# First tile's two top levels as one 64x128 matmul for both chunks, with another opening of zeros products

## The chip, the cores and the metric

The kernel runs on one core of one Trainium2 chip. The metric is the time of one execution in microseconds of device time. TensorE multiplies matrices, VectorE (DVE) and ScalarE (ACT) work on elements, GpSimd (POOL) helps with sums and masks, and SyncE (SP) issues most transfers.

## The reference

The inputs r, k, v and w have the shape (4, 8, 768, 48): batch, heads, time, head dimension. A recurrence over time gives y, and its heads side by side are the input of an MLP with an exact GELU.

```python
for t in range(S):
    kt, vt, rt, wt = (k[:, :, t], v[:, :, t], r[:, :, t], w[:, :, t])
    cur = np.einsum('bhd,bhe->bhde', u[None] * kt, vt)
    y[:, :, t] = np.einsum('bhd,bhde->bhe', rt, state + cur)
    state = wt[:, :, :, None] * state + np.einsum('bhd,bhe->bhde', kt, vt)
...
x = attn_out.transpose(0, 2, 1, 3).reshape(B * S, H * D)     # 3072 x 384
h = x @ w_in                                                 # 384 x 2048
g = 0.5 * h * (1.0 + erf(h * inv_sqrt2))
return g @ w_out                                             # 2048 x 384
```

## The kernel before

The work is cut into 8 tiles: four batches by two halves of the time axis, 384 steps each. A tile's attention is worked out in chunks of 64 steps. Inside a chunk, each product r·k with the decay between its two times is built up over levels of h = 1, 2, 4, 8, 16, 32 (`halves`, tiles 1 and 2): at level h the k of the left half of each block of 2h steps meets the r of its right half, then r and k are multiplied by the block's total decays (the updates, L617 and L628, on VectorE), and the block of the product that belongs to this level is copied into `a_sb`. Below h = 16 VectorE copies through a mask (L639); from 16 on ScalarE copies rectangles (L636). The diagonal (with u, prepared by ScalarE at L524) has a product of its own and a masked copy (L588). Updates of a level follow its product, since they overwrite what it reads, and the product of the next level follows the updates.

The first tile is treated alone: its eight heads fall into two units of four (`units[0]`, `units[1]`), each with `np_ = 1` of `NPART = 2` parts, so that unit 0 can start while unit 1's data is on its way. From level 2 on unit 1 goes ahead of unit 0. A level's product is made by `products` (L575): for each of the NI = 6 pairs of chunks, each head half g of the partitions and each chunk p of the pair one matmul of 64x64, whose operands are partitions `half[g]` of k and r and whose result lies in the partitions `half[p]` of a PSUM tile `d`. These are 24 fp32 matmuls. An fp32 matmul stands in the trace as two weight loads and two matmuls, a bf16 one as one of each. Behind the levels come the transposes of k (L798), copied by ScalarE (L800), the products kv (L824), the products of `a_sb` with v (L865), the chain of states on VectorE (L839), the products of r with the states (L894), and the copies into the MLP's input xT (L951, L967 and, over `ysb` with six small transfers, L970 and L886). Then TensorE starts the MLP of the first tile (L1084), interleaved with the second tile's levels.

`keep_warm` (L349) multiplies bf16 zeros into a bank that nobody reads. It opens the kernel with 12 products of 128 columns, followed by two fp32 ones of 512 columns (L353) while the first data is loaded; `products` calls it twice 512 columns behind the diagonals and behind levels 2 and 4 of the first tile, and the stream `warm` six times in the second tile.

The order on each engine is written out by hand: PLAN is a string per tile, whose letters advance streams (generators) of work, "." for unit 0, "s" for unit 1, "f" for the following tile, "l" for loads, "c" and "p" for the weights' conversion. Each engine works in the order in which its instructions were issued, with semaphores between engines; PSUM tiles `d` have three buffers.

Of the kernel before, what the change touches and what calls it, by code (L numbers as in the profile page):

```python
# [10 lines left out]
F32 = mybir.dt.float32  # L11
# [10 lines left out]
C = 64  # L22
# [6 lines left out]
NI = Q * N3  # L29
# [3 lines left out]
BANK = 512  # L33
# [159 lines left out]
def kernel(  # L193
# [9 lines left out]
    nc = tc.nc  # L203
    NX = rkw.shape[0]
    NP = u.shape[1]
    NPART = NP // Q
# [18 lines left out]
    def pair(name):  # L225
        return pools["d"].tile([128, 2, BANK], F32, name=name, tag="d")
# [14 lines left out]
    def bank(name="o_ps", i=None):  # L241
        if i is None:
            i = turns[0]
            turns[0] = 1 - i
        return ps.tile([128, BANK], F32, name=name, tag=f"m{i}")
# [3 lines left out]
    half = [slice(0, 64), slice(64, 128)]  # L249
# [84 lines left out]
    zeros = const.tile([128, BANK], BF16, name="zeros")  # L334
    nc.vector.memset(zeros, 0.0)
    long_zeros = zeros.bitcast(F32).unsqueeze(1).to_broadcast([128, 2, BANK // 2])
    two = const.tile([128, 1], F32, name="two")
# [5 lines left out]
    def keep_warm(n, elsewhere=False, n_cols=BANK):  # L343
        if elsewhere:
            t = pair("warm")[:, 0]
        else:
            t = bank("warm")
        for _ in range(n):
            nc.tensor.matmul(t[:, 0:n_cols], lhsT=zeros[:, 0:128], rhs=zeros[:, 0:n_cols], start=True, stop=True)  # L349

    keep_warm(12, n_cols=BANK // 4)
    for _ in range(2):
        nc.tensor.matmul(bank("warm"), lhsT=zeros[:, 0:2 * 128].bitcast(F32), rhs=long_zeros, start=True, stop=True)  # L353


    masks = {h: const.tile([128, C // 2], U8, name=f"mask{h}") for h in LEVELS if h < 16}
# [37 lines left out]
    for i, h in enumerate(QUARTERS[:1]):  # L394
        for a in range(3):
            w_q = (3 - a) * C // 4
            z = q_ints[1 if a == 0 else 2]
# [81 lines left out]
    def attention(x, unit):  # L479
# [3 lines left out]
        np_ = len(parts)  # L483
# [4 lines left out]
        r, k, w = (bufs[0 if x == 0 or i == 0 and x % 2 == 0 else 1][:, base + i * n_u:base + (i + 1) * n_u]  # L488
                   for i in range(3))
        rc, kc = (z.rearrange("p (b i c t) -> p b i c t", b=np_, c=2, t=C) for z in (r, k))  # L490
# [77 lines left out]
        def products(bs, right, width, warm=True):  # L568
            d = pair("d")
            n = 0  # L570
            for b in bs:
                for i in range(NI):
                    for g in range(2):
                        for p in range(2):
                            nc.tensor.matmul(d[half[p], g, n * width:(n + 1) * width],  # L575
                                             lhsT=kc[half[g], b, i, p], rhs=right(half[g], b, i, p),
                                             start=True, stop=True)
                    n += 1
            if x == 0 and warm:
                keep_warm(2)  # L580
            return d[:, :, 0:n * width]

        def diagonal():
            return [products([b], lambda z, b, i, p: rucs[b][z, i, p], C) for b in range(np_)]

        def copy_diagonal(diag):
            for b in range(np_):
                nc.vector.copy_predicated(out=at[:, :, b * NI:(b + 1) * NI],  # L588
                                          mask=masks[0].unsqueeze(1).unsqueeze(1).to_broadcast([128, 2, NI, C]),
                                          data=diag[b].rearrange("p g (i t) -> p g i t", t=C))  # L590

        def halves():

            for h in LEVELS:
                m = C // 2 // h
                if np_ < NPART:

                    d = products(range(np_), lambda z, b, i, p: rc[z, b, i, p], C, 1 < h < 8)
                    d = d.rearrange("p g (n m two j) -> p g n m two j", two=2, j=h, m=m)[:, :, :, :, 1, :]
                else:  # L600
                    right = rc.rearrange("p b i c (m two j) -> p b i c m two j", two=2, j=h)[:, :, :, :, :, 1, :]
                    d = products(range(np_), lambda z, b, i, p: right[z, b, i, p], C // 2)
                    d = d.rearrange("p g (n m j) -> p g n m j", j=h, m=m)
                if h == 1:
                    yield
                    diag = diagonal()
                yield

                r2 = r.rearrange("p (n two j) -> p n two j", two=2, j=h)[:, :, 1, :]
                t2 = tot[h].rearrange("p (n two) -> p n two", two=2)[:, :, 0:1].to_broadcast(r2.shape)  # L610
                k2 = k.rearrange("p (n two j) -> p n two j", two=2, j=h)[:, :, 0, :]
                tk = tot[h].rearrange("p (n two) -> p n two", two=2)[:, :, 1:2].to_broadcast(k2.shape)
                rk = bass.AP(tensor=r2.tensor, offset=r2.offset, ap=[r2.ap[0], [n_u - h, 2]] + list(r2.ap[1:]))
                tt = bass.AP(tensor=t2.tensor, offset=t2.offset, ap=[t2.ap[0], [1, 2]] + list(t2.ap[1:]))

                def update(z, r2=r2, t2=t2, k2=k2, tk=tk):
                    nc.vector.tensor_mul(*((k2, k2, tk) if z is k else (r2, r2, t2)))  # L617

                if x == 0 and m == 1:

                    update(k)
                    last_r.append(lambda: update(r))
                elif x == 0 and h == 1:
                    update(r)
                    yield
                    update(k)
                else:
                    nc.vector.tensor_mul(rk, rk, tt)  # L628
                yield
                ah = at.rearrange("p g n (m two j) -> p g n m two j", two=2, j=h)[:, :, :, :, 1, :]  # L630
                if h >= 16:

                    for p in range(2):
                        for i in range(m):
                            s = slice(p * 64 + i * 2 * h, p * 64 + i * 2 * h + h)
                            nc.scalar.copy(out=ah[s, :, :, i], in_=d[s, :, :, i])  # L636
                else:
                    mask = masks[h].rearrange("p (m j) -> p m j", j=h).unsqueeze(1).unsqueeze(1)
                    nc.vector.copy_predicated(out=ah, mask=mask.to_broadcast(ah.shape), data=d)  # L639
                if h == 1:  # L640
                    copy_diagonal(diag)
                yield
# [144 lines left out]

        last_r = []
        yield from halves() if x < 2 else quarters()


# [22 lines left out]
        def vs(b, i, g):  # L814
            o = ((parts[b] * NI + i) * 2 + g) * D
            return loaded[x][1][:, o:o + G]

        kvs = []
        for b in range(np_):
            kv_ps = pair("kv_ps")  # L820
            for i in range(NI):
                for p in range(2):
                    for g in range(2):
                        nc.tensor.matmul(kv_ps[half[g], p, i * D:(i + 1) * D], lhsT=k_t(b, i, p, g),  # L824
                                         rhs=vs(b, i, g)[half[p], 0:D], start=True, stop=True)
# [84 lines left out]
        else:  # L910
# [8 lines left out]
            for turn in range(2):  # L919
                for i in range(NI):  # L920
                    for b in range(np_):
                        p = (b + turn) % 2
                        for g in range(2):
                            nc.tensor.matmul(ys[turn][0][b][half[g ^ swap(b)], i * C:(i + 1) * C], lhsT=vs(b, i, g)[half[p]],
                                             rhs=at[half[p], g, b * NI + i, :], start=(i == 0), stop=True, skip_group_check=True)
# [7 lines left out]
            for turn in range(2):  # L933
                ysb = ysb_of() if turn == 0 else ysb
                a = ys[turn][1][:, :, 0:NI * C].rearrange("p b (q i t) -> p b q i t", q=Q, t=C)
                for z in range(2):
                    s = slice(z * G, z * G + D)
# [9 lines left out]
        if split:  # L947
            for c, copy in enumerate((nc.scalar.copy, nc.vector.tensor_copy)):
                for z in range(2):
                    s = slice(z * G, z * G + D)  # L950
                    copy(out=xT[s, 0:Q, :].rearrange("p q (i c t) -> p (q i) c t", c=2, t=C)[:, :, c, :],  # L951
                         in_=ys[0][0][c][s, 0:NI * C].rearrange("p (i t) -> p i t", t=C))
# [3 lines left out]
        for b in reversed(range(np_)):  # L956
            for q in reversed(range(Q)):
# [5 lines left out]
                if which < NJ:  # L963
                    for z in range(2):
                        s = slice(z * G, z * G + D)
# [291 lines left out]

    def warm():
        for _ in range(2):
            keep_warm(3, True)  # L1260
            yield

    def masks_and_sums():
# [6 lines left out]
    for x in range(NX):  # L1270
        following = attention(x + 1, 0) if x + 1 < NX else iter(())
        if x == 0:
            streams = {
                ".": units[0], "s": units[1], "f": following, "c": pieces_of_w, "w": next_v(), "x": warm(),
                "p": prepare_apart(),
                "l": chain(weight_in(0, True), islice(second, 5), weight_in(1, True), second, weight_in(2, True)),
            }
        else:
            streams = {
                **(mlp(x - 1) if x > 1 else {".": first_mlp()}),  # L1280
                "s": slots, "f": following,
                "l": load(x + 1, nc.sync),
                "x": sums_of_x(x),
                "w": masks_and_sums() if x == 1 else chain(h_sums([1]), o_sums(EARLY, len(FORMS_O))) if x == 2 else iter(()),
                "y": o_sums(0, EARLY) if x == 1 else iter(()),
                "c": pieces_of_w if x == 1 else iter(()),
            }
        for c in PLAN[x]:
            next(streams[c], None)
        for c in ".slxwp" if x == 0 else ".slxwcy" if x == 1 else ".vgeoslxw":  # L1290
            while next(streams[c], streams) is not streams:
                pass
        slots = following
        if x == 1:
            fewer_pairs()
# [63 lines left out]
```

## Time and profile before

| what | value |
|---|---|
| three timed runs | 575.67, 576.38, 577.77 us; median 576.38 |
| the profiled execution | 577.52 us, span 575.7 us, granted clock 1.00 |
| TensorE matmuls | busy 551.3 us (96%), 7412 instructions |
| TensorE weight loads | busy 491.1 us (85%), 7420 instructions |
| VectorE | busy 489.2 us (85%) |
| ScalarE | busy 334.1 us (58%) |
| first product of the MLP (L1084) | starts at 42.58 us |
| opening, L349 and L353 | 1.19 to 6.17 us |

Times in the trace count from the start of the span. A matmul's record includes a fixed time to drain, so that records of a dense row overlap; how often they start is their pace. PE is TensorE's matmul row, PEld its row of weight loads.

### The profile page before, as it was taken

The page shows a single profiled execution, that of the slowest core. Times are in us where ns is not written, and L with a number is a line of the kernel's source. Part 1 is how long each engine was busy: PE and PEld are TensorE (multiplying, and loading weights), DVE is VectorE, ACT ScalarE, POOL GpSimd, SP SyncE. Part 2 cuts the span into 40 slices and gives each one's busy share as a digit, 9 for nine tenths or more (in the row PEclk, how much of TensorE's full clock was granted, in tenths as well). Part 3 has the DMA queues.
Part 4 walks back from the last instruction along what each step waited for, and adds up shares of the span by engine and source line. Part 5 has one row for each costly group of instructions (what it writes and reads, how often), then busy time and mean ns, then how long its engine had stood idle before and what let it go on. Part 6 is the DMA issues. An engine that isn't in the chain of part 4 may idle for free. (4 is left out here: it accounts for less than half of the span.)

```text
span 575.7 us, 17712 instructions
## 1 busy us (share of the span) xinstructions
PE 551.3 (96%) x7412; PEld 491.1 (85%) x7420; DVE 489.2 (85%) x977; ACT 334.1 (58%) x768; POOL 106.1 (18%) x105
## 2 busy tenths in 40 slices
PE   7689999999998999999999999999999999999997
PEld 4576665689998989999898998989898988999997
DVE  7889879999989989798989979799888989755464
ACT  2468995347753677347763477527772478535820
POOL 5100000016200460006400252005500072000000
PEclk9999999999999999999999999999999999999999
DMA  8559742239342782558623593337915384200001
GB/s 303 178 159 370 239 142 87 81 86 154 47 82 64 175 106 36 139 156 131 81 46 114 135 165 44 60 91 159 131 30 135 84 105 62 43 25 30 0 1 41
DMA packets 71646, 62.15 MB, mean 108 GB/s; under 512 B 32912, under 2 KB 56720, under 8 KB 71568
## 3 DMA queue, kind: packets, MB, share of 16 engines
q1 hardware_dynamic: 50112, 45.62, 26.4%
q0 software_dynamic: 21216, 15.34, 20.3%
q8 instruction: 58, 0.95, 0.7%
q14 instruction: 20, 0.16, 0.1%
q10 hardware_dynamic: 240, 0.08, 0.1%
HBM read 36.24 MB, written 4.72 MB: 71 GB/s over the span
## 5 line engine op out<-in xcount | busy, mean ns | idle before, releaser
L1148 POOL DMA_DIRECT2D g<-o_sb x78 | 94.9, 1490 | 370.7 <-ACT g L1117 347.2
L1197 DVE TENSOR_TENSOR g<-g 128x512 f32<-128x512 f32 x112 | 75.1, 688 | 24.3 <-PE o_ps L1073 21.3
L1117 ACT COPY o_sb<-u_ps 128x384 f32<-128x384 f32 (+1 forms) x56 | 25.8, 461 | 67.6 <-PE u_ps L1073 66.2
L1073 PE MATMUL h_ps<-forms_x,w_in_sb 128*128 128x192 f32 x280 | 57.7, 332 | 0.0
L1073 PE MATMUL o_ps<-w_out_sb,g 128*128 128x192 f32 x280 | 50.5, 327 | 0.5 <-DVE g L1197 0.5
L1117 ACT COPY g<-h_ps 128x384 f32<-128x384 f32 x84 | 40.4, 482 | 16.3 <-PE h_ps L1073 14.4
L1073 PEld LDWEIGHTS h_ps<-forms_x,w_in_sb 128*128 128x128 f32 x280 | 46.6, 190 | 2.7 <-ACT g L1117 2.2
L1073 PEld LDWEIGHTS o_ps<-w_out_sb,g 128*128 128x128 f32 x280 | 46.0, 190 | 1.2 <-DVE g L1197 0.8
L1166 ACT ACTIVATE g<-g 128x384 f32<-128x384 f32 x98 | 46.2, 519 | 0.3
L1073 PE MATMUL o_ps<-t,g 128*128 128x192 f32 x224 | 41.4, 328 | 0.1
L726 ACT COPY a_sb<-d 32x320 f32<-32x320 f32 (+5 forms) x108 | 39.3, 364 | 3.6 <-DVE a_sb L784 1.7
L1073 PEld LDWEIGHTS o_ps<-t,g 128*128 128x128 f32 x224 | 36.8, 190 | 0.7 <-PE u_ps L1073 0.3
L1073 PE MATMUL h_ps<-forms_x,s 128*128 128x192 f32 x168 | 35.5, 334 | 0.0
L1073 PE MATMUL h_ps<-xT,w_in_sb 128*128 128x192 f32 x168 | 35.0, 331 | 0.1
L710 PE MATMUL d<-kx,rkw 64*64 64x96 f32 x1152 | 32.0, 248 | 3.0 <-ACT a_sb L726 1.9
L710 PEld LDWEIGHTS d<-kx,rkw 64*64 64x64 f32 x1152 | 25.6, 133 | 9.6 <-issue 4.3
L1084 PE MATMUL h_ps<-xT,w_in_sb 128*128 128x384 f32 x96 | 33.0, 494 | 0.2
L1073 PE MATMUL u_ps<-xT,w_in_sb 128*128 128x192 f32 x168 | 32.5, 328 | 0.1
L1073 PE MATMUL u_ps<-w_out_sb,g 128*128 128x192 f32 x168 | 30.9, 332 | 1.4 <-ACT o_sb L1115 0.8
L1092 PE MATMUL o_ps<-w_out_sb,g 128*128 128x384 f32 x96 | 31.7, 489 | 0.0
L575 PEld LDWEIGHTS d<-rkw 64*64 64x64 f32 x1152 | 19.1, 134 | 14.2 <-issue 8.5
L739 DVE COPY_PREDICATED a_sb<-quarter,d 128x480 f32<-128x480 uint8 (+5 forms) x54 | 23.2, 440 | 8.7 <-PE d L710 7.4
(178 smaller groups left out, 1206.2 us busy)
## 6 DMA issues: line engine op xcount, KB each, us to landing
g<-o_sb POOLq DMA_DIRECT2D x78, 192.0 KB, 4.2
rkw<-in_rkw_dram SPq DMA_DIRECT2D x54, 256.0 KB, 3.7
raw<-in_w_out_dram SPq DMA_DIRECT2D x8, 768.0 KB, 5.4
v_in<-in_v_dram SPq DMA_DIRECT2D x8, 584.0 KB, 4.6
out_dram<-o_sb SPq DMA_DIRECT2D x24, 192.0 KB, 2.1
raw<-in_w_in_dram SPq DMA_DIRECT2D x5, 768.0 KB, 9.2
rkw<-kx SPq DMA_DIRECT2D x72, 48.0 KB, 2.1
rkw<-in_rkw_dram SPq DMA_DIRECT2D x6, 384.0 KB, 6.8
```

The lines of the kernel that those rows point to most:

```text
L575: nc.tensor.matmul(d[half[p], g, n * width:(n + 1) * width], lhsT=kc[half[g], b, i, p], rhs=right(half[g], b, i, p), start=True, stop=True)
L710: nc.tensor.matmul(d[half[p], g, i * 3 * C // 2:(i + 1) * 3 * C // 2], lhsT=kc[half[g], n // NI, n % NI, p], rhs=rx[half[g], 2 * n + p], s ...
L726: nc.scalar.copy(out=at[z, g, first:behind, (a + 1) * h:], in_=d[z, :, :, to] if g == slice(None) else d[z, :, to])
L739: nc.vector.copy_predicated(out=an[:, :, :, :, (a + 1) * h:], mask=mask.to_broadcast(data.shape), data=data)
L1073: nc.tensor.matmul(o, lhsT=lhsT, rhs=rhs, start=start, stop=True, skip_group_check=True)
L1084: nc.tensor.matmul(h_ps, lhsT=w_in_sb[:, f // FI, j, f % FI * 128:(f % FI + 1) * 128], rhs=xT[:, j, :], start=(j == 0), stop=(j == NJ - 1))
L1092: nc.tensor.matmul(o, lhsT=gs[f // FG][:, f % FG, i * 128:(i + 1) * 128], rhs=w_out_sb[:, f, :], start=(f == 0), stop=(f == NF - 1))
L1117: nc.scalar.copy(out=o, in_=z)
L1148: nc.gpsimd.dma_start(out=o, in_=saved[q, t], accum_op=ALU.add)
L1166: nc.scalar.activation(out=o, in_=z, func=AF.Gelu, scale=MINUS.get(h, 1.0))
L1197: nc.vector.tensor_add(o, o, g_block(what[3:5]))
```

## The change

It has three parts.

The opening: instead of 12 bf16 products of 128 columns and two fp32 products of 512 columns, one fp32 product of 512 columns and then 59 fp32 products of 64x64 zeros, which go round the four quarters of the array in the order of the real products.

The two top levels of the first tile: for h = 16 and 32, `products_of_both` makes one matmul for both chunks of a pair. Its stationary operand is the k of both chunks (128 columns), its moving operand the right halves of r of both (64 columns). A unit's level takes 12 matmuls of 64x128 instead of 24 of 64x64. Half of each result belongs to k of one chunk and r of the other, and is not read; ScalarE's copies pick the matching chunk `p`.

The warming: `products` warms only behind the diagonals, no more behind levels 2 and 4, and the second tile's six warming products have 64 columns instead of 512.

```diff
-    keep_warm(12, n_cols=BANK // 4)
-    for _ in range(2):
-        nc.tensor.matmul(bank("warm"), lhsT=zeros[:, 0:2 * 128].bitcast(F32), rhs=long_zeros, start=True, stop=True)
+    nc.tensor.matmul(bank("warm"), lhsT=zeros[:, 0:2 * 128].bitcast(F32), rhs=long_zeros, start=True, stop=True)
+    small = zeros.bitcast(F32)
+    t = [bank("warm") for _ in range(2)]
+    for i in range(59):
+        g, p = half[i // 2 % 2], half[i % 2]
+        nc.tensor.matmul(t[i // 2 % 2][p, 0:64], lhsT=small[g, 0:64], rhs=small[g, 64:128], start=True, stop=True)
...
+        def products_of_both(h):
+            d = pair("d")
+            for i in range(NI):
+                for g in range(2):
+                    right = r[half[g], i * 2 * C:(i + 1) * 2 * C].rearrange("p (m two j) -> p m two j", two=2, j=h)[:, :, 1, :]
+                    nc.tensor.matmul(d[:, g, i * C:(i + 1) * C], lhsT=k[half[g], i * 2 * C:(i + 1) * 2 * C], rhs=right,
+                                     start=True, stop=True)
+            return d[:, :, 0:NI * C].rearrange("p g (n c m j) -> p g n c m j", c=2, j=h, m=C // 2 // h)
...
-                if np_ < NPART:
-
-                    d = products(range(np_), lambda z, b, i, p: rc[z, b, i, p], C, 1 < h < 8)
+                both = np_ < NPART and h >= 16
+                if both:
+                    d = products_of_both(h)
+                elif np_ < NPART:
+
+                    d = products(range(np_), lambda z, b, i, p: rc[z, b, i, p], C, False)
...
-                            nc.scalar.copy(out=ah[s, :, :, i], in_=d[s, :, :, i])
+                            nc.scalar.copy(out=ah[s, :, :, i], in_=d[s, :, :, p, i] if both else d[s, :, :, i])
...
-            keep_warm(3, True)
+            keep_warm(3, True, 64)
```

## The prediction

> **What bounds the kernel now.** I read the page first. TensorE is busy 96% of the span, and the table of stretches shows where the rest is:
>
> ```profile
> 42.60:110.00 67.40, 67.22 (x945) 42.94 (x942) 61.35 (x98) 53.87 (x80) 0.00 (x0) 1.00 0.53 184
> ```
>
> The first number after the stretch is its length, the next TensorE's busy time: from 42.6 us on TensorE has no holes to speak of, so the end of the kernel moves by as much as the first product of the MLP (L1084, at 42.58) moves. All that is changed runs before it. There TensorE has holes, and the timeline calls the larger ones "issue", a wait for nothing that the profile shows:
>
> ```profile
> 13.19 0.80 PE L575 MATMUL d<-rkw 64*64 64x64 f32 x38 [0.24 <-issue]
> ...
> 18.12 0.45 PE L575 MATMUL d<-rkw 64*64 64x64 f32 x11 [1.46 <-issue]
> ...
> 22.68 1.39 PE L575 MATMUL d<-rkw 64*64 64x64 f32 x80 [0.61 <-issue]
> ...
> 33.98 0.86 PE L865 MATMUL y_ps<-a_sb,v_in 64*64 64x64 f32 x44 [1.39 <-issue]
> ...
> 37.71 1.59 PE L575 MATMUL d<-rkw 64*64 64x32 f32 x94 [0.57 <-issue]
> ```
>
> Two lines of the page explain them:
>
> ```profile
> PE 551.3 (96%) x7412; PEld 491.1 (85%) x7420; DVE 489.2 (85%) x977; ACT 334.1 (58%) x768; POOL 106.1 (18%) x105
> ...
> q8 instruction: 58, 0.95, 0.7%
> ```
>
> A queue named "instruction" moves 58 packets, 0.95 MB, so 16 KB each; 7412 matmuls and 7420 weight loads over 58 packets are 256 instructions a packet. The stretches between the ends of those holes hold just that many (x after PE and PEld; an instruction across a border counts twice):
>
> ```profile
> 13.19:18.12 4.93, 3.18 (x125) 2.35 (x128) 4.75 (x9) 2.94 (x3) 3.67 (x7) 1.00 0.83 258
> 18.12:22.68 4.56, 3.40 (x125) 2.48 (x127) 3.69 (x9) 0.00 (x0) 0.00 (x0) 1.00 0.71 234
> 22.68:26.41 3.73, 2.32 (x129) 2.17 (x128) 3.58 (x7) 2.15 (x7) 0.00 (x0) 1.00 0.26 72
> 26.41:30.25 3.84, 3.49 (x126) 3.13 (x126) 2.77 (x7) 2.48 (x7) 0.00 (x0) 1.00 0.72 217
> ```
>
> So TensorE's program arrives in blocks of 256, one in use and one ahead: the trace starts a packet 1.1 to 1.4 us after a hole ends (2.1 to 2.4 while the DMA share is over 0.7), it takes 0.9 to 1.4 us, and the next block runs 1.2 to 1.5 us later. One block thus takes 3.7 us in quiet, 4.6 to 5.2 under load, while TensorE could run 256 such instructions in 1.9 us (48 matmuls and 48 loads in 0.93 less a drain of 0.22). Blocks begin at instruction 187 (run at 8.04) and then every 256, released at 13.19, 18.12, 22.68, 26.41, 30.25, 33.98, 37.71, 41.30. Beside this, VectorE is nearly full from 8 to 18 us. Past 36 us the path goes over ScalarE:
>
> ```profile
> 36.10 0.48 ACT L970 COPY ysb<-y_ps 128x384 f32<-128x384 f32 x1 [1.79 <-PE y_ps L894]
> 36.61 2.20 ACTq L886 DMA_DIRECT2D xT<-ysb  x3
> 38.90 0.96 ACT L951 COPY xT<-y_ps 48x384 f32<-48x384 f32 x2 [2.32 <-DVE xT L951]
> 39.87 2.14 ACT L524 ACTIVATE kx<-rkw,u_sb 128x384 f32<-128x384 f32 x4
> ```
>
> It waits for unit 1's states (L894), and these stand behind unit 0's y product, which the hole before 33.98 holds up.
>
> **The change in instructions.** An fp32 matmul is two loads and two matmuls, a bf16 one a load and a matmul. The opening grows from 12x2 + 2x4 = 32 to 4 + 59x4 = 240: plus 208. Four pairs of warming matmuls go (16), and four products (levels 16 and 32, two units) shrink from 24x4 to 12x4 (192): minus 208. From the transposes (L798) on, every block therefore begins where it did; before that, all of them fall earlier in the work:
>
> - 443: was 16 instructions into level 2's first product, now 5 into unit 1's level 1.
> - 699: was in level 4's first product, now 65 of 96 into level 2's first.
> - 955: was in level 8's second, now 33 into level 4's second.
> - 1211: was at level 32's first, now at level 16's first.
>
> **Opening.** TensorE starts at 1.19. The one long product takes two of the four records that now fill 2.44 to 6.17, 1.9 us. A small product's record takes 14.6 ns at the pace of L575; before 6.5 us the trace runs at half pace (128-column bf16 every 107 ns, 512-column ones later every 216), so 29 ns, 118 records in 3.4 us: done at 6.5, before the data (6.93). Cost 0, or 0.3 if each takes a tenth longer.
>
> **Blocks.** Instruction 187 is now the 46th small product, at 5.8 instead of 8.04. Before, 5.15 us lay between it and block 443, so 10.9; the fetch looks some 64 instructions ahead (in unbroken runs a packet starts 0.6 us after its border, not 1.1), worth 0.4 us more among slow products: 10.6. Unit 1's level 1 loses 1.1 us (its data allows 9.51). VectorE feels it at the k update (L617), which follows the diagonal product: 12.3 for 11.60, plus 0.7. Level 2's first product starts at 13.2, stops at instruction 699 until 10.6 + 4.93 = 15.5 and ends at 16.0; its update (L628) starts at 16.05 for 14.34, plus 1.7. Then VectorE works its queue off without the 0.15 and 0.46 us waits of before: level 4's first update at 19.55 for 18.66, plus 0.9. Block 955 comes at 15.5 + 4.56 = 20.1, level 4's second update at 20.85 for 20.03, plus 0.8; level 8's second 24.1 for 23.43; level 16's second 26.3 for 25.65, plus 0.65. Block 1211 (20.1 + 3.73 = 23.85) stops nobody, so level 32's first product, held until 26.41 before, starts at 26.45 behind its update and is done at the same 27.35. What was lost early is paid back here: at 28 us the shift is 0, within 0.1.
>
> The gain comes behind it. Block 1467 is there at 27.6 instead of 30.25. The fetch passes that border at about 29.0, while the kv products (L824) still wait for ScalarE, so block 1723 comes at 29.0 + 3.7 = 32.7 for 33.98. Unit 0's y product ends at 33.5, unit 1's states take 1.17 + 0.22: L970 at 35.0 for 36.10, minus 1.1. If L951 really waits for VectorE's L951 (38.89), which follows unit 0's states and the chain that ends at 35.43, only 0.8 of it comes through. I take **minus 0.9**.
>
> **Width.** No row has 64x128 fp32. Two such products fit beside each other where four 64x64 did, so 24 records of 58.3/2 ns are the same 0.70 us. That is one bound; 54.4 ns each (half the 108.7 between the 128-column transposes of L798), 1.31 us, is the other, and it would delay levels 16 and 32, in series on each unit, by 0.6 each, 1.05 where VectorE does not cover it. Below 0.70 the 58.3 ns excludes. I take 0.70, the nearest row in partitions and moving columns. The Trainium skill ("TensorE: Matmul & The Clock Gate", LDWEIGHTS) says that a load's time goes by its columns, P/1.2 ns; by it the loads would set 1.28 us and the sum become about plus 0.1. The rows of 64 and 128 columns (133 and 190 ns) go that way but not in proportion.
>
> **Rest at nothing.** The four removed warming pairs (about 0.5 us each) lay beside waits for blocks or VectorE: 0 to minus 0.1. Tile 2's six narrower ones stand ahead of diagonal products that wait for L524 until 42.02: 0. ScalarE's copies (L636) keep shape and number.
>
> **Sum.** The profiled execution took 577.52 (span 575.7 and 1.8 around it): minus 0.9 is 576.6. It lay 1.1 above the median of 576.38, which becomes **575.5**. A measurement can tell about 0.5%, 2.9 us, from no change.
>
> **Rivals.**
> - *128-column loads set the pace*: plus 1.05 on the sum, 576.5. For it the 190 ns row; against it that loads overlap matmuls all over the trace. 0.17.
> - *The first block comes later still*: the DMA engines are full from 2.7 to 15 us, and the first packet of before was the slowest. Half a us more, and a fetch that does not run ahead of waiting instructions (no gain at 33.98): 576.9. 0.15.
> - *It doesn't do what I say*: the holes are no fetches, so moving instructions moves none; only the warming is saved, 576.3. The Trainium skill ("Runtime: NRT & Kernel Launch", Instruction fetch mechanics) supports that: the next 16 KB page is fetched during the current one and crossing a border is "mostly hidden". The counts of 256 above speak against hidden. 0.08.
> - *More gain*: the first packet starts after 1.2 us as in quiet. Block 443 then stops nobody and the later ones come 1.2 us earlier: 574.2 or, with VectorE's waits gone too, 573.0. 0.16.
> - *Slower: TensorE falls back to half pace.* Between 13.7 and 20.1 us it now has holes of 1.9 and 2 us and no warming between. All through before, the granted clock stays 1.00 over holes of up to 1.5 us. It decides if some 3 us hold too little work: then about 5 us of products on the path between 20 and 37 us double, 575.5 + 5 = 580.5. The Trainium skill (same clock page, Part 1) closes the gate after one idle window of about 3.4 us; no run here has shown that, and no hole reaches it. 0.08.
>
> **Numbers.** The forecast has 0.36. The range of 573.2 to 577.9 holds it and all rivals but the last and the far end of more gain, with the spread of the runs (575.67 to 577.77) around the ends. Faster by over 0.5% (below 573.5) is half of "more gain", 0.08; slower (above 579.3) is half pace and a little for an unseen cost, 0.09; within, 0.83.
>
> **What would show it.** Right: holes that end near 10.6, 15.5 and 20.1, none before level 32, the y hole ending near 32.7, L970 at 35.0, L1084 at about 41.7. Wrong: holes still at 13.2 and 18.1 (no fetches), L636's products over 1 us (loads), L575 records 29 ns apart after 15 us (clock), or L1084 at 42.6 or later.

## The result, and the profile after

The change made the kernel slower: 581.52 us median of 9 runs (579.46 to 583.32) for 576.38 (575.39 to 578.82, 9 runs), a ratio of 1.0081 with a 95% interval of 1.0059 to 1.0104. The forecast was 575.5 with a range of 573.2 to 577.9. The profiled execution took 583.02 us (span 581.2); its mean granted clock (the share of TensorE's full speed that it was given) was 0.994, and 0.992 over the nine runs, where before's profile had 1.000. A border, below, is the place between two blocks of 256 instructions.

TensorE's timeline of the changed kernel, at the places that answer to the holes shown before (start, length, work; in brackets the idle time ahead of it and what ended that; L578, L880 and L1099 are L575, L865 and L1084 of before, L591 is the new product):

```profile
11.44 0.86 PE L578 MATMUL d<-rkw 64*64 64x64 f32 x43 [1.75 <-issue]
...
18.04 3.38 PE L578 MATMUL d<-rkw 64*64 64x64 f32 x110 [3.54 <-issue]
...
26.33 5.60 PE L591 MATMUL d<-rkw 64*128 64x64 f32 x96 [0.31 <-DVE rkw L643]
...
37.22 0.86 PE L880 MATMUL y_ps<-a_sb,v_in 64*64 64x64 f32 x44 [0.91 <-issue]
...
45.09 2.15 PE L578 MATMUL d<-kx,rkw 64*64 64x64 f32 x69 [0.47 <-issue]
47.16 3.21 PE L1099 MATMUL h_ps<-xT,w_in_sb 128*128 128x384 f32 x7
```

The second hole starts 34 matmul records into unit 1's level 2, where the prediction put instruction 699, but it ends at 18.04 and not at 15.5. Level 2's first update on VectorE follows it at 18.87. First the changed kernel, then before:

```profile
18.87 0.96 DVE L643 TENSOR_TENSOR rkw<-rkw,tot_sb 128x768 f32<-128x768 f32 x1 [3.22 <-PE d L578]
```

```profile
14.34 0.97 DVE L628 TENSOR_TENSOR rkw<-rkw,tot_sb 128x768 f32<-128x768 f32 x1
```

Of this delay of 4.5 us only a part is won back. The transposes of k start 3.7 us late (31.86 for 28.16), and ScalarE's rows stand 3.2 us behind those of before:

```profile
39.34 0.48 ACT L985 COPY ysb<-y_ps 128x384 f32<-128x384 f32 x1 [1.30 <-PE y_ps L909]
...
43.12 2.13 ACT L527 ACTIVATE kx<-rkw,u_sb 128x384 f32<-128x384 f32 x4
```

Between that row and the MLP's first product another 1.3 us is lost: 47.16 for 42.58 is 4.6. The stretches by the clock's own edges show what else happened (length, TensorE's busy time, ..., the clock last but two):

```profile
14.45:17.86 3.41, 0.05 (x1) 0.00 (x0) 1.17 (x3) 2.63 (x3) 1.48 (x4) 1.00 0.65 196
17.86:21.27 3.41, 3.23 (x110) 3.16 (x110) 2.16 (x5) 0.00 (x0) 0.00 (x0) 0.50 0.18 36
41.76:45.17 3.41, 1.99 (x92) 1.63 (x88) 3.21 (x8) 3.00 (x6) 0.00 (x0) 1.00 0.56 156
45.17:48.58 3.41, 3.41 (x71) 2.71 (x71) 2.78 (x6) 2.98 (x4) 0.00 (x0) 0.50 0.98 305
```

The clock was halved twice, each time for 3.41 us: behind the hole (0.05 of 3.41 us busy), and again behind a stretch that was busy for 1.99 of 3.41 us, in which TensorE waited for L527 and for a block. The second time takes the diagonal products and the first of the MLP (45.17 to 48.58). Behind the MLP's start TensorE is as full as before, and the rest of the loss there is small: the distance to before is 4.75 us when the MLP's second product starts (L1107, 90.51 for 85.76) and 5.5 at the end, after one stop at 407 us (1.14 us, a wait for ScalarE) that before's profile does not have.

### The profile page after: what moved, and what is told of

It reads as the page before. It is cut to its first block, busy times and chain, and to the rows that moved or that the text cites. A ratio compares the mean times of both kernels' runs of the same rounds, so it can differ in the third digit from the quotient of the medians.

```text
span 581.2 us, 17720 instructions
## 1 busy us (share of the span) xinstructions
PE 555.3 (96%) x7420; PEld 497.2 (86%) x7420; DVE 488.6 (84%) x977; ACT 333.2 (57%) x768; POOL 105.2 (18%) x105
## 4 chain that ended last, share of the span: by engine, by line
PE 68%; DVE 11%; issue 8%; ACT 7%; DMA 3%; SPq 1%; POOL 1%; ACTq 0%; DVEq 0%; POOLq 0%
PE u_ps L1088 18%; PE o_ps L1088 16%; PE h_ps L1088 11%; PE h_ps L1099 6%; PE o_ps L1107 5%; PE d L578 3%; ACT a_sb L741 3%; PE d L725 2%; DMA rkw<-in_rkw_dram 2%; DVE a_sb L754 2%; PE kv_ps L839 2%; PE y_ps L909 1%; PE y_ps L939 1%; DMA g<-o_sb 1%; DVE a_sb L799 1%
## 5 line engine op out<-in xcount | busy, mean ns | idle before, releaser
L1132 ACT COPY g<-h_ps 128x384 f32<-128x384 f32 x84 | 40.2, 480 | 16.5 <-PE h_ps L1088 14.5
L1099 PE MATMUL h_ps<-xT,w_in_sb 128*128 128x384 f32 x96 | 33.4, 500 | 0.0
L1107 PE MATMUL o_ps<-w_out_sb,g 128*128 128x384 f32 x96 | 31.7, 489 | 0.0
L1088 PEld LDWEIGHTS h_ps<-forms_x,s 128*128 128x128 f32 x168 | 27.7, 190 | 3.8 <-ACT u_ps L1132 3.8
```

The lines of the kernel that those rows point to most:

```text
L1088: nc.tensor.matmul(o, lhsT=lhsT, rhs=rhs, start=start, stop=True, skip_group_check=True)
L1099: nc.tensor.matmul(h_ps, lhsT=w_in_sb[:, f // FI, j, f % FI * 128:(f % FI + 1) * 128], rhs=xT[:, j, :], start=(j == 0), stop=(j == NJ - 1))
L1107: nc.tensor.matmul(o, lhsT=gs[f // FG][:, f % FG, i * 128:(i + 1) * 128], rhs=w_out_sb[:, f, :], start=(f == 0), stop=(f == NF - 1))
L1132: nc.scalar.copy(out=o, in_=z)
```

## The experiments

Fourteen kernels, each beside runs of the kernel before on the same chip (576.6 to 577.7 us median there). Clock is the mean granted clock over the runs; one stretch of 3.41 us at half pace lowers it by 0.0029. The kernel before did not always keep its clock either: of its 94 runs beside these kernels 31 had 0.997 or less, and the mean by chip was 0.998 to 1.000. The last columns come from each kernel's one profile: level 2's first update, and the MLP's first product.

| kernel | us (runs) | ratio, 95% interval | clock | level 2 update | MLP start |
|---|---|---|---|---|---|
| before (its profile) | 577.52 (1) | | 1.000 | 14.34 | 42.58 |
| the change | 581.52 (9) | 1.0081 (1.0059 to 1.0104) | 0.992 | 18.87 | 47.16 |
| opening only | 582.81 (7) | 1.0088 (1.0055 to 1.0122) | 0.993 | 17.89 | 47.89 |
| 64x128 products only | 580.56 (12) | 1.0055 (1.0028 to 1.0081) | 0.998 | 14.23 | 42.87 |
| less warming only | 576.72 (12) | 0.9970 (0.9947 to 0.9994) | 0.996 | 14.76 | 44.53 |
| change, old opening | 580.53 (11) | 1.0053 (1.0019 to 1.0086) | 0.993 | 14.41 | 41.58 |
| fp32 opening of 32 instructions | 578.29 (10) | 1.0003 (0.9979 to 1.0027) | 0.998 | 14.26 | 44.05 |
| change, fewer zeros | 588.17 (1) | | 0.988 | 16.13 | 47.89 |
| change, loads held | 586.99 (1) | | 0.985 | 15.72 | 49.64 |
| opening, four loads later | 581.38 (10) | 1.0075 (1.0048 to 1.0101) | 0.994 | 15.61 | 45.98 |
| change, old opening, borders restored | 589.73 (1) | | 0.983 | 14.09 | 49.46 |
| short opening, less warming | 579.37 (1) | | 0.997 | 13.95 | 42.51 |
| narrow later warming only | 578.73 (12) | 1.0019 (0.9993 to 1.0045) | 0.997 | 14.21 | 42.15 |
| no warming at levels 2 and 4 only | 577.31 (12) | 0.9984 (0.9954 to 1.0014) | 0.995 | 14.11 | 41.13 |
| change, filled hole | 583.75 (6) | 1.0103 (1.0077 to 1.0128) | 0.997 | 17.52 | 44.89 |
| opening, filled hole | 583.10 (12) | 1.0084 (1.0056 to 1.0113) | 0.997 | 17.78 | 48.31 |

**Which part costs the time.** The first four take the change apart.

Opening only:

```diff
+    nc.tensor.matmul(bank("warm"), ..., rhs=long_zeros, ...)
+    for i in range(59): ...                       # small zeros products, as in the change
     # warming and 64x64 products as before
```

> The kernel before with the new opening alone (59 small zeros products, all warming kept, 64x64 products at every level). Theory A (the opening adds 208 instructions, so every border between instruction blocks of 256 comes earlier in the work, while the fetches cannot come earlier because the first loads hold the DMA engines until about 15.6 us): TensorE stands from about 14.3 to 18 us as after the whole change, level 2's first update comes at 18.5 to 19 us instead of 14.3, the granted clock halves for 3.4 us behind the hole, the first MLP product starts at 45.5 to 47 us instead of 42.6, and the time is 579 to 581 us. Rival R1 (the clock and the wait come from the warming taken out): no half pace, 576 to 577 us. Rival R2 (the 64x128 products cost it): 576 to 577 us.

Measured 1.0088, all of the loss and a little above Theory A's numbers (582.81 us, MLP start 47.89). The hole and the clock are much like those of the whole change, although all warming is kept:

```profile
13.55 0.79 PE L578 MATMUL d<-rkw 64*64 64x64 f32 x34
17.07 0.70 PE L578 MATMUL d<-rkw 64*64 64x64 f32 x14 [2.73 <-issue]
```

```profile
13.33:16.75 3.42, 0.90 (x35) 0.65 (x34) 2.12 (x5) 2.40 (x3) 2.81 (x8) 1.00 0.73 236
16.75:20.16 3.41, 2.73 (x63) 2.02 (x65) 0.97 (x2) 0.42 (x1) 0.00 (x0) 0.50 0.35 96
```

Warming could not help: its instructions stand behind the same border.

64x128 products only:

```diff
-                if np_ < NPART:
+                both = np_ < NPART and h >= 16
+                if both:
+                    d = products_of_both(h)
+                elif np_ < NPART:
```

> The kernel before with one 64x128 product for both chunks at levels 16 and 32, opening and warming as before. Theory A: the borders up to level 16 stay where they were, nothing before level 16 moves; each of the four products takes 1.26 us instead of 0.70, of which between 0 and 2.2 us in all reach the MLP's start; 192 instructions fewer move the later borders; no half pace; 576 to 578.5 us. Rival R2: the products are the loss, 579 to 582 us. Rival R1: 576.4 us.

The time is what R2 expected (580.56), above Theory A's range. But in the profile the products themselves are little of the loss: level 2 is where it was and the MLP starts 0.3 us late. The profiled run (579.54 us) ends 2.0 us behind before's, so most of that lies behind the MLP's start (below).

Less warming only:

```diff
-                    d = products(..., C, 1 < h < 8)
+                    d = products(..., C, False)
-            keep_warm(3, True)
+            keep_warm(3, True, 64)
```

> The kernel before without the warming behind levels 2 and 4 and with 64 columns in the second tile's six warming products. Theory A: holes end at 13.2 and 18.1 us as before and stay below 3.4 us, so the clock does not fall at 18 us; around 41 to 45 us TensorE may fall to half pace once for 3.4 us, worth up to 1.7 us; 576 to 578 us. Rival R1 (the missing warming behind levels 2 and 4 lets the clock fall at 18 us): half pace between 18 and 22 us, 578 to 581 us.

It is the only kernel here whose interval lies below 1, by 1.7 us at the middle and next to nothing at the end. The clock did halve once in its profile, at 13.63 us; Theory A had it fall, if at all, at 41 to 45 us. The MLP starts 1.95 us late in this profile, and 1.4 us of that is gone by the end: what is lost ahead of the MLP does not pass on whole in every kernel.

The change with the old opening:

```diff
-    nc.tensor.matmul(bank("warm"), ..., rhs=long_zeros, ...)
-    for i in range(59): ...
+    keep_warm(12, n_cols=BANK // 4)
+    for _ in range(2): nc.tensor.matmul(bank("warm"), ..., rhs=long_zeros, ...)
```

> The changed kernel with the old opening (12 bf16 products and two long fp32 ones): 64x128 products and less warming stay. Theory A: the first borders are back where they were, the hole ends at 18.1 us after less than 2 us, no half pace there; level 2's first update at 14.3 to 14.5 us; what stays is the 64x128 products' 0.56 us each and at most one half-paced stretch at 42 to 46 us: 576 to 579 us. Rivals R1 and R2 (warming, width): the loss stays, 580 to 582 us.

The front is as Theory A has it (update at 14.41, MLP 1.0 us earlier than before), the time is that of the rivals. Its runs spread with the clock: 577.58 and 578.50 us at 0.997 and 1.000, 585.19 and 586.02 at 0.985 and 0.984. So the parts other than the opening have costs of their own; they come out under "The loss behind the front".

**Number or kind.** An opening of fp32 zeros only, as long as the new one, with 32 instructions:

```diff
-    keep_warm(12, n_cols=BANK // 4)
     for _ in range(2): nc.tensor.matmul(bank("warm"), ..., rhs=long_zeros, ...)
+    for i in range(6):
+        nc.tensor.matmul(t[i // 2 % 2][p, 0:256], lhsT=small[g, 0:64], rhs=small[g, 0:256], ...)
```

> The kernel before with an opening of fp32 zeros products only, as long as the new one but of 32 instructions as the old one: two of 512 columns and six 64x64 quarters of 256 columns. Theory A (it is the 208 instructions): all borders stay, holes end at 13.2 and 18.1 us as before, first MLP product at 42 to 43.5 us, granted clock 0.997 or more; ratio 0.998 to 1.003. Rival R3 (the kind of product, fp32 zeros in place of bf16, leaves TensorE slower or the clock lower): first MLP product at 46 to 48 us, ratio 1.006 to 1.011.

The hole is shorter than before's, and the ratio is 1.0003: fp32 zeros do no harm, 208 more instructions do.

```profile
17.63 0.45 PE L579 MATMUL d<-rkw 64*64 64x64 f32 x11 [0.92 <-issue]
```

(The MLP's start, 44.05, lies outside what was expected; one half-paced stretch behind the y hole, at 36.05 us, is in this profile.)

The change with 124 instructions fewer:

```diff
+    nc.tensor.matmul(bank("warm"), ..., rhs=long_zeros, ...)      # a second long one
-    for i in range(59):
+    for i in range(27):
```

> The changed kernel with 27 small zeros products instead of 59 and a second long one in their place: about the same TensorE time in the opening, 124 instructions fewer. Theory A (number of instructions and the loads): border 699 lies 124 instructions later in the work, the second packet still starts at 14.5 to 15.7 us and its block runs at 17 to 18.2 us, so that the hole ends where it ended but begins about 2 us later (about 16 us), is shorter than 2.5 us, and the clock does not halve behind it; level 2's first update at 14 to 15 us, first MLP product at 42 to 44 us; 576 to 580 us. Rival R3 (the kind of product in the opening, not their number, is what counts): hole from 14.3 to 18 us, half pace, first MLP product at 46 to 48 us, 580 to 583 us.

The time, 588.17 us, fits neither theory, and the MLP's start, 47.89, is where Rival R3 had it. Block 699 stopped TensorE for only 0.15 us, and the update came at 16.13 instead of 18.87. But the clock halved earlier (at 12.13, in the first hole, which ends at 12.46), the borders behind the levels now fell into the products y and with the states (holes up to 34.41 and 37.86 us), and half pace followed from 42.85 to 53.09 us. It is a single run, which ends 10.7 us behind before's profile: moving borders moves the holes, and fewer instructions alone are not a remedy.

**What holds the packet.** The trace's instruction queue gives when a packet starts, the timeline when its block runs:

| kernel | first packet, block runs | second packet, block runs |
|---|---|---|
| before | 10.88, 13.19 | 15.62, 18.12 |
| the change | 9.00, 11.44 | 15.56, 18.04 |
| opening only | 8.88, 11.28 | 14.55, 17.07 |
| change, loads held | 8.89, 11.05 | 12.21, no stop |
| opening, four loads later | 9.13, 11.44 | 12.60, 15.02 |
| opening, filled hole | 8.75, 11.20 | 13.41, no stop |

```diff
-    0: "l.s....llsl.lssslslss.lc.l.slslls...
+    0: ".s....s.ssssss.llllllllc.l.slslls...       # the change, loads held
+    0: "l.s....lls.ssssss.lllllc.l.slslls...       # opening only, four loads later
```

> The changed kernel with the first eight loads of weights and of the second tile moved behind the levels in the first tile's order; nothing else moves. Theory A (the loads hold the second packet back): the second packet starts 1.1 to 1.5 us after the first hole's end (12.3 to 13.3 us) instead of 4.1 us, its block runs by 15.0 to 16.0 us, level 2's first update comes at 15.5 to 16.5 us, and no window of 3.4 us is empty, so no half pace at 18 us. The time itself may well be worse, since the weights come later. Rival R4 (the packets are late for a reason of their own, such as a fixed time after the border): second packet at 15.5 us and hole to 18 us as after the change.

> The kernel before with the new opening (240 instructions), and the second tile's first four loads issued a few steps later in the first tile's order. Theory A (new opening moves the borders up, the loads hold the packet): the second packet starts at 12.3 to 13.5 us instead of 14.6, its block runs by 16 us instead of 17.1 us, level 2's first update at 15 to 16.5 us; the window in which the clock was lost is used more, so the half pace at 16.7 us goes in most runs; first MLP product 1.5 to 4 us earlier than with the opening alone (47.9 us), ratio 1.000 to 1.006. Rival R4 (late for a reason of its own): as the opening alone, ratio 1.007 to 1.011, first MLP product at 47 to 48 us.

With the loads out of the way the second packet starts 1.2 us after the end of the first hole, as in quiet stretches, and with the loads held level 2 runs through:

```profile
14.00 2.29 PE L578 MATMUL d<-rkw 64*64 64x64 f32 x96
```

With the loads in place, over all kernels, it starts 1.6 to 4.1 us after the hole. So Theory A's packet is shown, against R4. But the time did not come back in either: 1.0075 is R4's range (its MLP start, 45.98, is Theory A's), and the first, a single run, though the clock no longer fell at 18 us, lost it at 12.03 and at 25.68. In the second kernel the loads that were moved met the next packet but one:

```profile
15.02 0.45 PE L578 MATMUL d<-rkw 64*64 64x64 f32 x14 [0.53 <-issue]
...
25.00 1.24 PE L578 MATMUL d<-rkw 64*64 64x64 f32 x37 [2.22 <-issue]
```

```profile
21.04:24.45 3.41, 1.25 (x72) 1.01 (x62) 2.58 (x5) 0.00 (x0) 0.00 (x0) 1.00 0.94 285
24.45:27.86 3.41, 2.86 (x104) 2.86 (x103) 2.30 (x4) 0.95 (x4) 0.00 (x0) 0.50 0.66 220
```

The packet started late (22.78 us, DMA share 0.94), the hole moved from level 2 to a later level, and with it the half pace.

**Late block or half pace.** Four long zeros products ahead of unit 1's level 2 give TensorE something to do in the hole:

```diff
+                if x == 0 and h == 2 and unit == 1:
+                    for _ in range(4):
+                        nc.tensor.matmul(bank("warm"), ..., rhs=long_zeros, ...)
```

The first has it on the change, the second on the opening alone, in place of the warming at levels 2 and 4, so that no later border moves.

> The changed kernel with four fp32 zeros products of 512 columns (16 instructions, about 3.5 us of TensorE) ahead of unit 1's level 2, so that the hole in front of the late block is filled with work that nobody needs. The block comes no earlier. Theory A1 (the late block itself is most of the loss, the half pace behind it a small part): TensorE still stops short of 18 us, level 2's first update at 18.2 to 18.9 us, no half pace there; first MLP product at 46 to 47.2 us for 47.16; ratio 1.005 to 1.009. Theory A2 (the half pace behind the hole is most of it): first MLP product at 42.5 to 45 us, ratio 0.999 to 1.004.

> The kernel before with the new opening, and with the four warming pairs behind levels 2 and 4 replaced by four fp32 zeros products of 512 columns ahead of unit 1's level 2: as many instructions as with the opening alone, but TensorE has work in the hole. Theory A1 (the late block itself is the loss): half pace at 16.7 us gone, granted clock 0.997 or more in most runs, and still ratio 1.005 to 1.009, first MLP product at 45 to 47.5 us. Theory A2 (the half pace behind the hole is the loss): ratio 0.999 to 1.004, first MLP product at 42.5 to 45 us.

The second kernel's timeline and stretch:

```profile
13.18 3.60 PE L600 MATMUL warm<-zeros 128*128 128x512 f32 x8
16.71 1.63 PE L578 MATMUL d<-rkw 64*64 64x64 f32 x96
```

```profile
13.77:17.18 3.41, 3.41 (x38) 1.46 (x40) 1.59 (x3) 2.86 (x3) 2.38 (x7) 1.00 0.66 172
```

The half pace at 17 us is gone in both, and the loss stays (1.0103 and 1.0084). On the change, three runs at a clock of 0.999 to 1.000 still took 581.67, 583.50 and 583.68 us. (In the first two, some 1 us more than in the others lies outside the span, which is 579.0 and 580.5 us.) The twelve runs of the second have a mean clock of 0.997, hardly below the 0.998 of before's runs beside them. So a level 2 that starts at 16.5 or later costs time with the clock kept. It is not shown that the late block alone would: the packet came earlier in these two (13.39 and 13.41), and the filling itself stood in the way until 16.45 and 16.71. Both MLP starts, 44.89 and 48.31, lie outside the numbers of Theory A1 (46 to 47.2, 45 to 47.5), and the first, inside A2's, was not followed by A2's time.

**The loss behind the front.** The 64x128 products alone leave out 192 instructions (with the old opening and less warming, 208), and every later border falls elsewhere. First the 64x128 kernel, then before, at the first tile-2 products of r with the states:

```profile
102.24 1.57 PE L906 MATMUL y_ps<-rkw,st 64*64 64x64 f32 x95
105.03 0.21 PE L906 MATMUL y_ps<-rkw,st 64*64 64x64 f32 x1 [1.21 <-issue]
```

```profile
101.59 1.58 PE L894 MATMUL y_ps<-rkw,st 64*64 64x64 f32 x96
103.10 4.14 PE L1092 MATMUL o_ps<-w_out_sb,g 128*128 128x384 f32 x12
```

A border now falls on the last product of a row of small ones, and TensorE stands for a block. It does so again at 245, 378 and 510 us; before has its own such stops, at other places (178 and 445 us). On TensorE, this profile is 0.6 us behind before at 88 us, 2.1 behind after the first of these stops, and 2.0 behind at the end. To test it, 208 instructions of zeros went into the first MLP of the change with the old opening:

```diff
         for f in range(NF):                      # first MLP, 13 of its 16 block rows
+            for p in 2 * half if f < 13 else ():
+                nc.tensor.matmul(t[p, T:T + 64], lhsT=small[half[0], 0:64], rhs=small[half[0], 64:128], ...)
             for j in range(NJ):
```

> The changed kernel with the old opening, and 52 zeros products of 64x64 (208 instructions) spread over the first 13 block rows of the first MLP: every border from 80 us on lies where it lay before. Theory A (the loss of the two runs with the old opening and 64x128 products comes from borders that fell into later rows of small products): from 100 us to the end this kernel keeps its distance to the kernel before within 0.7 us, without the steps of 0.5 to 1.5 us at 102, 242 to 246, 375 and 505 us; first MLP product at 41.5 us, the added products take 1 to 3 us; 576 to 578.5 us. Rival R5 (those steps are accidents of a run): steps of such size stay, at other places, 577.5 to 581 us.

From 123 us to the end its distance to before goes from 12.0 to 12.2 us. The border stops at 102, 245, 378 and 510 us are gone; the row that stopped at 105.03 now runs through:

```profile
113.55 1.58 PE L908 MATMUL y_ps<-rkw,st 64*64 64x64 f32 x96
```

One step of 1.4 us remains near 236 us, a wait for VectorE, which others give back. It is one profile. What was not foreseen is the front, and with it the time (589.73): MLP start at 49.46. Here the clock halved at 19.44 and stayed so for 17.07 us, through all four 64x128 products (line, engine, tile: shortest, median and longest record in ns):

```profile
L590 PEld LDWEIGHTS d<-rkw x96: 283/331/331, 22.9 to 32.9; 64*128 64x128 f32 x96
```

```profile
22.86:33.10 10.24, 10.24 (x99) 10.23 (x96) 3.92 (x7) 3.41 (x10) 0.00 (x0) 0.50 0.39 109
```

They take 10.2 us here and 5.6 at full pace, and while they run the clock does not come back. The kernel with the loads held had the same from 25.68 to 39.34. So in these two profiles a half pace that meets the 64x128 products lasts four to five times as long. That would explain why the times of the change with the old opening follow its clock; its own profile, at a clock of 1.000, does not show it.

**Less warming, by parts.** Three kernels look for a version that is faster:

```diff
+    keep_warm(3)                # for 12 of 128 columns, with less warming as above
...
+            keep_warm(3, True, 64)              # alone
...
+                    d = products(..., C, False) # alone
```

> The kernel before without the warming behind levels 2 and 4, narrow warming in the second tile, and with 3 bf16 products of 512 columns instead of 12 of 128 in the opening: 34 instructions fewer in all, so borders 34 instructions later in the work. Theory A: the front's holes are no longer than before, first MLP product at 41.5 to 44.5 us; the later borders cost at most 1 us more than before: 575 to 578 us. Rivals have no different number for it.

> The kernel before with only the second tile's six warming products narrowed to 64 columns. Theory A: no border moves; six products of 216 ns in front of the diagonal products go, so the first MLP product starts 0 to 1.2 us earlier; with the clock kept, ratio 0.997 to 1.000. Rival R1 (the warming is what keeps the clock there): half pace for 3.4 us at 42 to 48 us in most runs, mean granted clock 0.997 or less, ratio 1.000 to 1.004.

> The kernel before without the warming behind levels 2 and 4; opening, 64x64 products and the second tile's wide warming as before. Theory A (taking out 16 instructions moves the early borders 16 later in the work and frees 1.7 us of TensorE in the front, the clock is kept by the products themselves): first MLP product 0 to 1.5 us earlier, ratio 0.994 to 0.999. Rival R1 (that warming keeps the clock): granted clock below 0.997 in most runs, ratio 1.000 to 1.005.

The single run of the first was no gain (579.37 beside 576.57), above what was expected. Narrowing the later warming starts the MLP 0.4 us earlier in the profile and costs clock (0.997 or less in 9 of 12 runs, against 7 of before's 29), as the rival had it; its ratio, 1.0019, is not told apart from no change. Without warming at levels 2 and 4 the MLP starts 1.4 us earlier; the clock is lower too (0.995), and 0.9984 is not told apart from no change. Both together (0.9970) is the one version that beat the kernel before and the changed one, at the edge of what can be measured.

## Why the prediction was wrong

**Blocks: right in kind, wrong in the second time.** The borders fell where the instruction count put them: a first hole a few instructions into unit 1's level 1, a second two thirds through unit 1's level 2. The first block ran at 11.44 for 10.6. The second was reckoned as "10.6 + 4.93 = 15.5", as if the time from one block to the next were a property of the fetch. It was not: the packet waited under the loads, 4.1 us from the end of the first hole where the 4.93 us hold a wait of 2.4, and started at 15.56, where it had started before (15.62). The block ran at 18.04 for 18.12 before, with 208 instructions less of real work in front of it. This term, 2.5 us (0.8 of them from the first block, 1.7 from the longer wait), is the main error. The prediction had the reason in its hands: it noted DMA engines that are full to 15 us, and made of it half a microsecond on the first packet in a rival.

**Give-back: did not come.** The forecast let the shift fall from 1.7 at level 2 to 0 at 28 us, because block 1211 had held level 32 before. From 4.5 us it fell only to 3.7 at the transposes. Then "block 1723 comes at 29.0 + 3.7 = 32.7" failed as well: the border ahead of it was crossed by the kv products, which came with the late work at 33.6, so the y hole ended at 37.22, and the 1.1 us of gain became 3.2 us of loss.

**Half pace: the right rival, with the wrong point and too small a chance.** It had 0.08, "if some 3 us hold too little work". It came in every one of the nine runs, one to four stretches in each by their clocks (0.996 to 0.988). Its direct part in the profile is small where the prediction put it: 14 records at 29 instead of 14.6 ns ahead of level 2's first update, 0.2 us, and 0.24 us that the second update waited. The larger part is the second stretch, which the prediction did not have: 69 diagonal records took 2.15 us where 1.23 would do at full pace, 0.9 of the 1.3 us lost between L527 and the MLP. Between runs of the kernel before, one stretch more goes with 1.4 to 1.9 us more (a straight line through its runs on each of four chips), yet the change's own nine runs do not follow their clock (579.46 us at 0.988, 583.02 at 0.994). The filled holes show that a late level 2 costs as much with the clock kept; how the loss of the change itself divides between the late block and the half pace stays open.

**Width: took the wrong bound, with little effect.** Taken at 0.70 us a product, "the nearest row"; measured 5.60 for four, 1.40, beyond the other bound of 1.31. The products of the two head halves do start 7 ns apart, but the next pair starts 112 ns after them, not 58.3. The Trainium skill ("TensorE: Matmul & The Clock Gate", LDWEIGHTS) has a load's time go by its columns; an estimate from it, with the loads of the two halves side by side, is 1.28 us, close to the 1.40. In the profiles of the whole change it hardly shows: with 64x64 products (opening only) the transposes start at 31.60, with 64x128 at 31.86.

**Rest at nothing: not so.** Narrower warming in tile 2 was put at 0; alone it lowers the clock in most runs. That no border behind the MLP's start moves was right for the whole change: its counts cancel, and the profile shows no new border stops there. Only the partial kernels paid for them.

**Opening at cost 0:** right as TensorE's time (first real product at 6.37 for 6.93, the diagonal products behind it done at 8.61 for 8.56), wrong as instructions.

## What to carry to other kernels

Where an engine's program arrives in blocks, instructions are a resource of their own: filler ahead of the data costs no time of the engine here and still uses up a block, and while the loads fill the DMA engines the next one comes late. Count instructions up to the busiest DMA stretch before anything is added there, and fill a wait with few long instructions (32 of them cost nothing here, 240 cost 5 us), not many short ones. Test parts of a change with the later borders kept in place, since a part by itself can lose some 2 us in rows of code that it does not touch.

## What the runs showed of the hardware

- **The clock.** All half-paced stretches are multiples of 3.41 us (3.41, 10.24, 13.65, 17.07), on one grid in each run. A stretch need not be empty: the clock fell behind 0.05, 0.90 and 1.25 us of TensorE busy in 3.41. Over all sixteen profiles every stretch at full pace with less than 1.4 us busy was followed by half pace. From 1.46 to 2.19 us some were and some were not: it fell behind 1.99 (the change) and 2.19 (fewer zeros, 39.44 to 42.85), and was kept behind 1.46 (filled hole, 573.93 to 577.34), 1.61 (fewer zeros, 32.61 to 36.02) and 1.91 (before, 16.77 to 20.18). So the busy time of one stretch does not decide it alone in that range. The Trainium skill ("TensorE: Matmul & The Clock Gate", Part 1) has the window of 3413 ns, free-running, and the fall after an idle one; the length and the grid agree, but a part-used window was enough here.
- **Wide loads with little to move** (64x128 stationary, 64 columns moving) fill TensorE's record (10.24 us busy of 10.24) and yet left the clock at half in two profiles, within stretches of 13.65 and 17.07 us. Begun at full pace, they kept it (the change, 26.33 to 31.86).
- **Instruction packets** start 1.2 us after a block's release in quiet and 1.6 to 4.1 under the first loads. Why it was 13.4 in one kernel and 15.6 in another under the same loads was not settled. The Trainium skill ("Runtime: NRT & Kernel Launch", Instruction fetch mechanics) calls a border's crossing "mostly hidden"; here TensorE stood for up to 3.54 us at one.
